# Mirroring the first score group of each sequence into groups 3 to 5 of a fused attention and expert kernel

## The chip, the cores and the metric

One core of one Trainium2 chip runs the whole program. The metric is device time in microseconds of one execution; the time shown for a kernel is the median of several runs.

## What is computed

There are 8 sequences of 2816 tokens with 256 features. Attention has no softmax: squared, rectified scores of `z` with itself weight `v`, and `u` gates the result. The gated rows go to a mixture of experts: a dense two-layer block for every token, and one of eight experts, chosen by the largest logit and weighted by its probability.

```
scores = (1/S) * z @ z.T                  # per sequence, S = 2816, z has 64 features
x      = u * (relu(scores)**2 @ v)        # 22528 x 256 in all
y      = relu(x @ w1_dense) @ w2_dense
e, g   = argmax and its softmax weight of x @ w_gate
out    = y + g * (relu(x @ w1[e]) @ w2[e])
```

The scores of a sequence are a symmetric matrix. A block of it that was computed for keys i and queries j is, turned, the block for keys j and queries i.

## The kernel before

Tokens of a sequence lie in 22 blocks of 128. The query blocks of a sequence form six groups of widths 2, 4, 4, 4, 4, 4, here called 0 to 5; `groups` lists them for all sequences, and `n` counts them through, so that `n % 6` is the place in the sequence. For each group a tile `A[n]` holds the squared scores of all 22 key blocks against the group's queries, in bf16. There are three such tiles in turn (`bufs=3`), so group 3 of a sequence takes the buffer that group 0 had.

- `scores` (matmuls on line 390) makes score steps: for a group of width 4 a step is two key blocks, two matmuls with 64 rows each on the two halves of TensorE. `relu` gives each step two operations after it: an evacuation with scale and relu into `r` (line 405 on ScalarE, 407 on VectorE) and a squaring into `A[n]` (lines 418 and 420). A small list planner (`offer`, `best`, `give`, `run`) puts each on the engine that it expects to be free first; the order on TensorE, ScalarE, VectorE and SyncE is the order in which Python issues the instructions.
- `far[n]` names the groups whose scores group n takes over in place of computing them: before, only group n - 2 of the same sequence. `far_steps` makes the transposing DMA for it (line 468 on SyncE's queue, 16 blocks, or 8 from group 0), `turned_to` says where in `A[n]` it goes, and `block` finds a block again for the multiplication. The steps wait in the list `turning`; `av` takes one from it at fixed points of its loop, once the planner expects the source to be there. `open_group(n)` first carries out all steps of group n - 3, whose buffer it takes.
- `av` multiplies two query blocks of a group with `v` (line 579): 22 key blocks, twice, in pairs of 64-row matmuls. Between them `fill` puts score steps of the group itself or of the next two groups, when a pair of PSUM banks is free (four pairs rotate, `pairs`). `gate_x` (line 606) then multiplies with `u` into `pays` and turns the result by DMA (line 608) for the routing logits (line 634), which come every 11 blocks, five blocks late.
- `load_u` (line 146) loads `u` four blocks ahead on SyncE's queue. `load_z` (line 106) and `load_v` (line 129) are issued from GpSimd's queue, as are the scatters of gated rows (line 724) and the expert weights (`weights`, lines 255 and 259). The weights of all experts stay in one tile `wall`, 2048 columns (`WD`) for each expert. A small VectorE memset ahead of a load decides when it is issued.
- `turn_z` copies half of the next sequence's `z` on VectorE (line 113) and turns it by DMA on SyncE's queue (line 116).
- The table near the end gives ticks to these loads: tick `b * nK + x` is block x of sequence b. Before, the next `z` is loaded at block 0 and turned at blocks 5 and 6, `v` comes at blocks 13 to 18, and the dense and expert weights at blocks 15, 18 and 21, from sequence 1 to 7.

After attention (about 560 us) the experts run tile by tile on rows that were sorted by scatter. That part is not touched.

Of the kernel before, what the change touches and what calls it, by code (L numbers as in the profile page):

```python
# [15 lines left out]
P = 128  # L16
# [3 lines left out]
def kernel(  # L20
# [13 lines left out]
    B, S, D = u.shape  # L34
    dq = z.shape[2]
    E = moe_w_gate.shape[1]
    F = moe_w1_dense.shape[1]
    N = B * S
    assert D == 256 and dq == 64 and F == 512 and E == 8 and S % (2 * P) == 0
    nK = S // P  # L40
# [19 lines left out]
    WD = 2 * F + 4 * D  # L60
# [28 lines left out]
    wall = const.tile([P, E, WD], BF, name="wall")  # L89
# [13 lines left out]
    def load_z(b):  # L103
        z_of[b] = zpool.tile([P, nK, dq], BF, name="zr", bufs=1)
        nc.vector.memset(z_of[b][:, 0, 0:1], 0.0)
        nc.gpsimd.dma_start(out=z_of[b][:], in_=z[b].rearrange("(p k) d -> p k d", p=P))

    def turn_z(b, k0, k1):

        if k0 == 0:  # L110
            zn_of[b] = zpool.tile([P, nK, 2, dq], BF, name="zn", bufs=1)
            zT_of[b] = zpool.tile([P, nK, P], BF, name="zT")
        nc.vector.tensor_copy(
            zn_of[b][:, k0:k1, :, :],
            z_of[b][:, k0:k1, :].unsqueeze(2).to_broadcast([P, k1 - k0, 2, dq]))
        nc.sync.dma_start_transpose(
            out=zT_of[b][:, k0:k1, :],
            in_=zn_of[b][:, k0:k1].rearrange("p k h d -> p (k h d)"))
        if k1 == nK:
            z_there.add(b)  # L120

    def load_v(b, h, parts, gate=True):
        if h == 0:
            v_of[b] = zpool.tile([P, nK, D], BF, name="vb")
        src = v[b].rearrange("(p k) d -> p k d", p=P)
        k0, k1 = h * nK // parts, (h + 1) * nK // parts
        if gate:
            nc.vector.memset(v_of[b][:, k0, 0:1], 0.0)
        nc.gpsimd.dma_start(out=v_of[b][:, k0:k1, :], in_=src[:, k0:k1, :])
        free["pool"] = max(free["pool"], now[0]) + 0.8  # L130
# [133 lines left out]
    A = {}  # L264
    groups = []
# [16 lines left out]
    def offer(ready, rank, ways, then=None):  # L282
        count[0] += 1
        todo.append((rank, count[0], ready, ways, then))
# [56 lines left out]
        run(now[0])  # L341


    left, far, key_at = {}, {}, {}
    for n, (b, i0, w) in enumerate(groups):
        far[n] = [m for m in (n - 2,) if m >= 0
                  if groups[m][0] == b]
        turned = {k for m in far[n] for k in range(groups[m][1], groups[m][1] + groups[m][2])}
        ks = [k for k in range(0, nK, 2) if k not in turned]

        left[n] = [tuple(ks[x:x + 4 // w]) for x in range(0, len(ks), 4 // w)]

    def open_group(n):
        if n not in A:
            while turning and turning[0][0] <= n - 3:
                turning.pop(0)[1]()
            A[n] = aA.tile([P, nK, 4 * P], BF, name="A", tag="A")[:]
            w = groups[n][2]
            if w < 4:
                A[n] = A[n].rearrange("p k c -> p (k c)")[:, :nK * w * P]  # L360
                A[n] = A[n].rearrange("p (k c) -> p k c", k=nK)
# [81 lines left out]
    def turned_to(a, n):  # L443

        _, j0, wj = groups[a]
        w = groups[n][2]
        flat = A[n].rearrange("p k c -> p (k c)")
        return flat[:, j0 * w * P:(j0 + wj) * w * P]

    def block(n, k, c):  # L450

        _, i0, w = groups[n]
        for a in far[n]:
            _, j0, wj = groups[a]
            if j0 <= k < j0 + wj:
                x = c * wj + k - j0
                return turned_to(a, n)[:, x * P:(x + 1) * P]
        return A[n][:, k, c * P:(c + 1) * P]

    def far_steps(a):  # L460

        _, j0, wj = groups[a]

        def step(n):
            _, i0, w = groups[n]
            assert a + 1 in A
            open_group(n)
            nc.sync.dma_start_transpose(
                out=turned_to(a, n).rearrange("p (x c) -> p x c", c=P),
                in_=A[a][:, i0:i0 + w, :].rearrange("p k c -> p (k c)"))  # L470
            turn_at[0] = now[0] + 0.17 * w * wj
            read_at[a] = now[0] + 1.5 + 0.19 * w * wj
            for j in range(wj):
                key_at[n, j0 + j] = now[0] + 7.0

        return [(a, lambda n=n: step(n), n) for n in (a + 2,) if a in far.get(n, [])]

    turning = []
    turn_at = [0.0]
# [73 lines left out]
    def av(n, i, between):  # L553
        b, i0, w = groups[n]
        if i == i0:
            turning.extend(far_steps(n))
# [452 lines left out]
    def at(tick, fn):  # L1009
        later.setdefault(tick, []).append(fn)  # L1010

    def soon(t, fn, dur=0.07):
        at(t, lambda: offer(now[0], 3, {"dve": (dur, lambda eng: fn())}))

    def dense(w, src, c):
        nc.vector.memset(w[:, 0, 0:1], 0.0)
        nc.gpsimd.dma_start(out=w[:], in_=src.rearrange("(c p) f -> p c f", p=P))
# [3 lines left out]
    for b in range(B):  # L1021
        t = b * nK
        if b + 1 < B:
            soon(t, lambda b=b: load_z(b + 1))
            soon(t + 5, lambda b=b: turn_z(b + 1, 0, nK // 2), 0.4)
            soon(t + 6, lambda b=b: turn_z(b + 1, nK // 2, nK), 0.4)
            for h in range(8):
                soon(t + 13 + 5 * h // 7, lambda b=b, h=h: load_v(b + 1, h, 8))

    ts = [b * nK + x for b in range(1, B) for x in (15, 18, 21)][2:]  # L1030
    soon(ts.pop(0), lambda: dense(w1d, moe_w1_dense, 2))
    soon(ts.pop(0), lambda: dense(w2d, moe_w2_dense, 4))
    for e in range(E):
# [62 lines left out]
    for q in range(nQ - 2):  # L1096
        t = starts[q + 1] - 1 + LAG
# [40 lines left out]
    for s in range(NT - MAYBE + 2):  # L1138
# [4 lines left out]
        if s % 3 == 1 and waiting:  # L1143
# [5 lines left out]
    n = nc.values_load(used[0:1, 0:1], min_val=0, max_val=NH,  # L1149
                       skip_runtime_bounds_check_because="made by the table")  # L1150
# [34 lines left out]
```

## Time and profile before

| | before |
|---|---|
| runs | 885.04, 883.94, 883.76 us; median 883.94 us |
| profiled execution | 883.35 us, of it a span of 881.2 us from first to last instruction |
| granted TensorE clock | 0.997 of full speed |
| TensorE / VectorE / ScalarE / GpSimd busy | 861.5 / 700.9 / 737.2 / 491.6 us |
| DMA moved | 127.62 MB, 145 GB/s over the span |
| a sequence in the steady part | 67.43 us |

Busy times are sums over one profiled execution. The queues named SPq and POOLq only issue DMAs; the data moves later on 16 DMA engines that all queues share. A DMA share above 1 means that packets of several queues were under way on one engine at once, their times added.

### The profile page before, as it was taken

To read this page: it belongs to the slowest core of one execution; us is meant where nothing else is said; L and a number is where in the kernel's file an instruction comes from. 1 tells how busy PE (TensorE), PEld (TensorE's weight loads), DVE (VectorE), ACT (ScalarE), POOL (GpSimd) and SP (SyncE) were. 2 spreads that over 40 slices of the span, in tenths; PEclk is the share of its full clock that TensorE was granted. 3 is DMA by queue.
4 is the path that set the end of the run, shared out by engine and by line. 5 is a ranking of instruction groups with operands and counts; after the bars stand their busy time and mean duration, and the time that the engine had idled before them with its cause. 6 is when DMAs were issued, how large, how long until landed. Compare 5 with 4: busy or idle time off the path is not lost.

```text
span 881.2 us, 30493 instructions
## 1 busy us (share of the span) xinstructions
PE 861.5 (98%) x12257; PEld 757.7 (86%) x12257; DVE 700.9 (80%) x1348; ACT 737.2 (84%) x913; POOL 491.6 (56%) x560
## 2 busy tenths in 40 slices
PE   7999999999999999999999999999999999999995
PEld 5788898898888888888888888888888888889994
DVE  7999999998999999999999996756665445446663
ACT  7999998998998998998998994577777777777773
POOL 8203355445426436436336334588888888877664
PEclk9999999999999999999999999999999999999998
DMA  8897988979979979989999976465646565533442
GB/s 155 148 151 139 161 162 149 185 165 173 181 161 185 167 165 185 162 181 143 198 182 165 165 135 115 104 136 131 136 122 120 121 123 122 124 103 103 95 98 76
DMA packets 258830, 127.62 MB, mean 145 GB/s; under 512 B 222846, under 2 KB 237438, under 8 KB 258688
## 3 DMA queue, kind: packets, MB, share of 16 engines
q1 hardware_dynamic: 227040, 70.23, 46.2%
q0 software_dynamic: 31648, 55.45, 29.6%
q8 instruction: 96, 1.57, 0.8%
q14 instruction: 46, 0.38, 0.1%
HBM read 61.54 MB, written 37.16 MB: 112 GB/s over the span
## 4 chain that ended last, share of the span: by engine, by line
PE 81%; POOL 6%; issue 4%; DVE 4%; DMA 2%; ACT 1%; SPq 0%; POOLq 0%; DVEq 0%; ACTq 0%
PE o L579 44%; PE h_ps L936 13%; PE yy L944 12%; PE s L390 10%; POOL out_dram L962 5%; DMA out_dram<-ring,ix 1%; DVE r L407 1%; PE lg L634 1%; POOL A L420 1%; DVE A L420 1%; ACT r L405 1%; DMA ring<-xs 1%; DVE pays L606 0%; ACT A L418 0%; DMA z<-in_z_dram 0%
## 5 line engine op out<-in xcount | busy, mean ns | idle before, releaser
L579 PE MATMUL o<-vb,A 64*128 64x256 bf16 x7744 | 491.1, 269 | 3.3 <-POOL A L420 1.7
L579 PEld LDWEIGHTS <-A 64*128 64x128 bf16 x7744 | 406.5, 94 | 53.7 <-POOL A L420 3.0
L724 POOL DMA_INDIRECT xs<-pays,pi x176 | 190.2, 1081 | 249.3 <-DVE pi L722 204.5
L405 ACT ACTIVATE r<-s 128x1024 f32<-128x1024 f32 (+1 forms) x268 | 263.8, 1012 | 21.6 <-PE s L390 19.2
L418 ACT ACTIVATE A<-r 128x1024 bf16<-128x1024 f32 (+1 forms) x263 | 266.6, 1046 | 7.1 <-DVE r L407 4.2
L939 ACT ACTIVATE ring<-h_ps 128x1024 bf16<-128x1024 f32 x180 | 184.1, 1024 | 89.6 <-PE h_ps L936 88.1
L407 DVE TENSOR_SCALAR r<-s 128x1024 f32<-128x1024 f32 (+1 forms) x164 | 197.6, 1215 | 6.5 <-PE s L390 1.9
L420 DVE TENSOR_TENSOR A<-r 128x1024 bf16<-128x1024 f32 x161 | 196.4, 1231 | 2.1 <-ACT r L405 1.7
L960 DVE SCALAR_TENSOR_TENSOR ring<-yy,me,ring 128x256 f32<-128x256 f32 x180 | 86.9, 483 | 124.6 <-ACT ring L959 84.7
L962 POOL DMA_INDIRECT out_dram<-ring,me x140 | 147.5, 1054 | 42.0 <-issue 24.4
L390 PE MATMUL s<-zT 64*128 64x512 bf16 (+1 forms) x944 | 156.8, 357 | 1.8 <-ACT zT L192 0.6
L944 PEld LDWEIGHTS <-ring 128*128 128x128 bf16 x1440 | 140.1, 98 | 16.1 <-issue 0.3
L944 PE MATMUL yy<-w2d,ring 128*128 128x256 bf16 x720 | 108.0, 273 | 0.1
L944 PE MATMUL yy<-ring 128*128 128x256 bf16 x720 | 108.0, 273 | 0.0
L936 PE MATMUL h_ps<-ring,w1d 128*128 128x256 bf16 x720 | 93.3, 272 | 1.0 <-DVE pays L606 0.8
L936 PE MATMUL h_ps<-ring 128*128 128x256 bf16 (+1 forms) x880 | 93.7, 253 | 0.0
L924 DVE COPY ring<-wall 128x2048 bf16 x110 | 79.7, 740 | 8.0 <-DVE ring L960 4.0
L936 PEld LDWEIGHTS <-ring 128*128 128x128 bf16 x880 | 74.3, 98 | 6.8
L936 PEld LDWEIGHTS <-w1d 128*128 128x128 bf16 x720 | 70.1, 98 | 9.3 <-issue 1.0
L390 PEld LDWEIGHTS <-zT 64*128 64x128 bf16 x944 | 57.6, 94 | 16.5 <-issue 2.6
L606 DVE TENSOR_TENSOR pays<-o,ut 128x512 bf16<-128x512 f32 x88 | 60.4, 687 | 14.0 <-PE o L579 13.7
L959 ACT COPY ring<-yy 128x256 f32<-128x256 f32 x180 | 65.9, 366 | 1.8 <-PE yy L944 1.8
(120 smaller groups left out, 370.0 us busy)
## 6 DMA issues: line engine op xcount, KB each, us to landing
ut<-in_u_dram SPq DMA_DIRECT2D x88, 256.0 KB
vb<-in_v_dram POOLq DMA_DIRECT2D x42, 192.0 KB
wall<-in_moe_w_dram POOLq DMA_DIRECT2D x16, 256.0 KB
xs<-pays,pi POOLq DMA_INDIRECT x176
zr<-in_z_dram POOLq DMA_DIRECT2D x7, 352.0 KB
out_dram<-ring,me POOLq DMA_INDIRECT x140
ring<-xs SPq DMA_TRANSPOSE x114
vb<-in_v_dram POOLq DMA_DIRECT2D x14, 128.0 KB
```

The costliest lines, as they stand in the source:

```text
L390: nc.tensor.matmul(out=s[:, h, y * c:(y + 1) * c], lhsT=zT[r, k + h, :], rhs=zT[r, i0:i0 + w, :], start=True, stop=True)
L405: nc.scalar.activation(r[:, :, :c], s[:, :, :c], AF.Relu, scale=1.0 / S)
L407: nc.vector.tensor_scalar(out=r[:, :, :c], in0=s[:, :, :c], scalar1=1.0 / S, scalar2=0.0, op0=ALU.mult, op1=ALU.max)
L418: nc.scalar.activation(a, r, AF.Square)
L420: (nc.gpsimd if eng == "pool" else nc.vector).tensor_mul(a, r, r)
L579: nc.tensor.matmul(out=o[:, j, 0:D], lhsT=block(n, k, i + j - i0)[r], rhs=v_of[b][r, k, :], start=(p == 0 and x == 0), stop=(p == 1 and x ...
L724: ins = nc.gpsimd.indirect_dma_start(out=xs, out_offset=bass.IndirectOffsetOnAxis(ap=pi[:], axis=0), in_=pays[:, g % (2 * G), 0:ROW].bitca ...
L936: nc.tensor.matmul(out=h_ps[:, f, hs, :], lhsT=w1(c, f), rhs=xT[:, hs, c, :], start=(c == 0), stop=(c == 1))
L939: nc.scalar.activation(h, h_ps[:].rearrange("p f h t -> p f (h t)"), AF.Relu)
L944: nc.tensor.matmul(out=y[:, k, :], lhsT=h[:, f, j * P:(j + 1) * P], rhs=w2(f), start=(f == 0), stop=(f == 3))
L960: nc.vector.scalar_tensor_tensor(out=ys, in0=y[:, 1, :], scalar=me[:, j, 0:1], in1=yd, op0=ALU.mult, op1=ALU.add)
L962: ins = nc.gpsimd.indirect_dma_start(out=out, out_offset=bass.IndirectOffsetOnAxis(ap=ids[j], axis=0), in_=ys, in_offset=None, bounds_chec ...
```

## The change

For every sequence but the last, the scores that group 0 computed (its two query blocks) are now turned into groups 3, 4 and 5 too, besides group 2, which had them before. Groups 3 to 5 then have one score step fewer each. `A` keeps its size: the three turned pieces, 128 x 1024 each, go into the columns of `wall` that belong to the last expert and to the second half of the one before. Those weights are loaded in the last sequence, at blocks 4, 9 and 14, when no mirror is made any more; the earlier weights keep their order. `z` of the next sequence is loaded three blocks sooner, at block 19 of the sequence before (at block 0 for the first), and turned at blocks 0 and 1 (5 and 6 in the first sequence).

```diff
+    spare = wall[:].rearrange("p e w -> p (e w)")
+    mirror = {(0, 4): (E - 1) * WD, (0, 5): (E - 1) * WD + 8 * P, (0, 3): (E - 2) * WD + 2 * F}
+
+    def slots(b):
+
+        return list(mirror) if b < B - 1 else []
...
-        far[n] = [m for m in (n - 2,) if m >= 0
-                  if groups[m][0] == b]
+        far[n] = [m for m in range(max(n - 5, 0), n - 1)
+                  if groups[m][0] == b and (m == n - 2 or (m % 6, n % 6) in slots(b))]
...
-        flat = A[n].rearrange("p k c -> p (k c)")
-        return flat[:, j0 * w * P:(j0 + wj) * w * P]
+        if a == n - 2:
+            flat = A[n].rearrange("p k c -> p (k c)")
+            return flat[:, j0 * w * P:(j0 + wj) * w * P]
+        x = mirror[a % 6, n % 6]
+        return spare[:, x:x + w * wj * P]
...
-            assert a + 1 in A
-            open_group(n)
+            if n == a + 2:
+                assert a + 1 in A
+                open_group(n)
...
-        return [(a, lambda n=n: step(n), n) for n in (a + 2,) if a in far.get(n, [])]
+        return [(a, lambda n=n: step(n), n) for n in range(a + 2, min(a + 6, len(groups)))
+                if a in far[n]]
...
-            soon(t, lambda b=b: load_z(b + 1))
-            soon(t + 5, lambda b=b: turn_z(b + 1, 0, nK // 2), 0.4)
-            soon(t + 6, lambda b=b: turn_z(b + 1, nK // 2, nK), 0.4)
+            soon(max(t - 3, 0), lambda b=b: load_z(b + 1))
+            tz = t if b else 5
+            soon(tz, lambda b=b: turn_z(b + 1, 0, nK // 2), 0.4)
+            soon(tz + 1, lambda b=b: turn_z(b + 1, nK // 2, nK), 0.4)
...
-    ts = [b * nK + x for b in range(1, B) for x in (15, 18, 21)][2:]
+    ts = [b * nK + x for b in range(1, B - 1) for x in (15, 18, 21)][2:-1]
+    ts += [(B - 1) * nK + x for x in (4, 9, 14)]
```

More of the change, by code (lines that the diff above doesn't have):

```diff
@@ L1023 @@
         if b + 1 < B:
-            soon(t, lambda b=b: load_z(b + 1))
-            soon(t + 5, lambda b=b: turn_z(b + 1, 0, nK // 2), 0.4)
-            soon(t + 6, lambda b=b: turn_z(b + 1, nK // 2, nK), 0.4)
+            soon(max(t - 3, 0), lambda b=b: load_z(b + 1))
+            tz = t if b else 5
+            soon(tz, lambda b=b: turn_z(b + 1, 0, nK // 2), 0.4)
+            soon(tz + 1, lambda b=b: turn_z(b + 1, nK // 2, nK), 0.4)
             for h in range(8):
                 soon(t + 13 + 5 * h // 7, lambda b=b, h=h: load_v(b + 1, h, 8))
-    ts = [b * nK + x for b in range(1, B) for x in (15, 18, 21)][2:]
+    ts = [b * nK + x for b in range(1, B - 1) for x in (15, 18, 21)][2:-1]
+    ts += [(B - 1) * nK + x for x in (4, 9, 14)]
+    assert len(ts) == 2 + 2 * E
     soon(ts.pop(0), lambda: dense(w1d, moe_w1_dense, 2))
```

## The prediction

> **What bounds the kernel now.** I read the page first (busy shares, the chain that ended last, the groups), then the waits of TensorE, then the busy time per stretch of one sequence, and last the single queues around the place where a sequence begins. The page:
>
> ```profile
> PE 861.5 (98%) x12257; PEld 757.7 (86%) x12257; DVE 700.9 (80%) x1348; ACT 737.2 (84%) x913; POOL 491.6 (56%) x560
> DMA  8897988979979979989999976465646565533442
> PE 81%; POOL 6%; issue 4%; DVE 4%; DMA 2%; ACT 1%; SPq 0%; POOLq 0%; DVEq 0%; ACTq 0%
> ...
> L579 PE MATMUL o<-vb,A 64*128 64x256 bf16 x7744 | 491.1, 269 | 3.3 <-POOL A L420 1.7
> ...
> L405 ACT ACTIVATE r<-s 128x1024 f32<-128x1024 f32 (+1 forms) x268 | 263.8, 1012 | 21.6 <-PE s L390 19.2
> L418 ACT ACTIVATE A<-r 128x1024 bf16<-128x1024 f32 (+1 forms) x263 | 266.6, 1046 | 7.1 <-DVE r L407 4.2
> ...
> L407 DVE TENSOR_SCALAR r<-s 128x1024 f32<-128x1024 f32 (+1 forms) x164 | 197.6, 1215 | 6.5 <-PE s L390 1.9
> L420 DVE TENSOR_TENSOR A<-r 128x1024 bf16<-128x1024 f32 x161 | 196.4, 1231 | 2.1 <-ACT r L405 1.7
> ...
> L390 PE MATMUL s<-zT 64*128 64x512 bf16 (+1 forms) x944 | 156.8, 357 | 1.8 <-ACT zT L192 0.6
> ```
>
> TensorE is busy 98% and holds 81% of the chain. The reader should see that its two attention groups have almost no idle time ahead of them (3.3 and 1.8 us in all), while ScalarE and VectorE, which turn scores into A, wait for it: 19.2 us of ACT's idle ends with a score. One sequence, in the steady stretches, beside the expert half (first column the stretch, then its length):
>
> ```profile
> core 0: us, PE busy (x) PEld busy (x) DVE busy (x) ACT busy (x) POOL busy (x), PEclk, DMA share, GB/s
> 253.79:321.22 67.43, 67.34 (x1150) 58.83 (x1148) 64.07 (x119) 63.30 (x70) 30.16 (x34) 1.00 0.93 173
> 388.65:456.08 67.43, 67.34 (x1150) 58.84 (x1148) 64.06 (x119) 63.30 (x70) 30.05 (x34) 1.00 1.04 172
> 560.00:881.00 321.00, 310.90 (x3009) 280.06 (x3007) 179.62 (x387) 228.57 (x357) 247.94 (x288) 0.99 0.51 115
> ```
>
> A sequence takes 67.43 us, 67.34 of them TensorE at full clock. So attention is bound by TensorE, with VectorE (64.07) and ScalarE (63.30) 5 to 6% behind. A stall of either for more than a moment stops TensorE, and the DMA share is near or over 1. The change touches attention alone; the expert stretch after 560 us keeps its 321 us.
>
> **What is removed.** In each of the first seven sequences, groups 3, 4 and 5 no longer compute the score step of key blocks 0 and 1: 3 x 7 = 21 steps, each two 64x512 matmuls that run beside each other, one evacuation with relu and one squaring. The order of the built program bears this out: 42 matmuls `s<-zT` fewer, 14 evacuations and one squaring fewer on DVE, 7 and 20 fewer on ACT. The matmul's mean of 357 ns is no price, since pairs overlap. The chain, piece by piece, has it:
>
> ```profile
> 258.68 0.22 PE s L390 x2
> 258.90 1.75 PE o L579 x32
> 260.64 0.22 PE s L390 x2
> ```
>
> A pair holds the chain for 0.22 us (a pair of A-times-v matmuls 1.75/16 = 0.109). So TensorE loses 21 x 0.22 = 4.6 us of work, or 0.66 us per sequence. On ACT and DVE 21 steps of about 2.14 us go (263.8+266.6+197.6+196.4 over 432 steps), 45 us in all. That is worth nothing by itself: those engines already wait for TensorE, which has only 0.09 us of idle left per sequence. Multiplying costs what it did: the same 7744 matmuls are issued, and 336 of them read the mirror instead of A.
>
> **What is added.** 21 transposing DMAs of 128x1024 on SP's queue (8 blocks, 262 kB each). In before's trace group 0's one transpose and what stands around it on SP, with the long transposes of group 1:
>
> ```profile
> 287.12 0.34 SPq L146 DMA_DIRECT2D ut<-in_u_dram  x1
> 287.56 1.23 SPq L608 DMA_TRANSPOSE xT<-pays  x1
> 288.89 1.29 SPq L468 DMA_TRANSPOSE A<-A  x1
> ...
> 296.00 4.26 SPq L468 DMA_TRANSPOSE A<-A  x1
> 300.35 0.54 SPq L146 DMA_DIRECT2D ut<-in_u_dram  x1
> ```
>
> Now four transposes come out of A of group 0 instead of one. Two DMAs that turn z, until now at blocks 5 and 6, move between them, and in the program's order group 1's transpose follows at once. What waits for that: (a) SP: group 1's transpose writes the buffer of group 0 and so waits until all four have read it, with the next u and xT behind it; u is asked for four blocks early and xT is used five blocks late, some 12 us each (67.43/22 a block), so this costs nothing below that. (b) ACT and DVE: group 3 uses group 0's buffer, so their first squaring into it waits for the last mirror. Behind it on ACT is the evacuation of the next score, and TensorE's routing logits take the PSUM pair which that frees. This is the one place where the change can cost TensorE time. (The mirrored keys are not needed before group 3 multiplies, over 10 us later.)
>
> I lay (b) out from the u load that opens this burst (time 0), placing each issue by the TensorE work ahead of it in the built program (0.109 and 0.22 as above). SP: u 0.3, xT 1.2, two mirrors of 1.29, to 4.2; half of z's turn waits for its copy on DVE and ends at about 5.8; mirror three to 7.1; u and xT of the next pair to 8.7; the last mirror is issued from 8.8 to 10.1. The data cannot come much faster than DMA moves it. The price of that, from half-microseconds around a 16-block transpose that has SP and DMA nearly to itself:
>
> ```profile
> 307.02 2.16 SPq L468 DMA_TRANSPOSE A<-A  x1
> ...
> 307.50:308.00 0.50, 0.50 (x9) 0.18 (x6) 0.43 (x3) 0.50 (x1) 0.08 (x1) 1.00 1.26 245
> 308.00:308.50 0.50, 0.50 (x10) 0.41 (x10) 0.50 (x1) 0.50 (x2) 0.50 (x1) 1.00 1.20 223
> ...
> 310.00:310.50 0.50, 0.50 (x14) 0.44 (x12) 0.46 (x4) 0.41 (x2) 0.00 (x0) 1.00 1.19 214
> 311.00:311.50 0.50, 0.50 (x14) 0.44 (x12) 0.50 (x2) 0.50 (x2) 0.50 (x1) 1.00 0.25 42
> ```
>
> That is about 230 GB/s, starting about 1 us after the issue. Ahead of the last mirror's end lie two u (524 kB), two xT (328), four mirrors (1049), half of z (360), one weight half (262) and two or three scatters (some 200), by their shapes: 2.7 MB, or 11.7 us. From 0.9 on that ends at 12.6. In ACT's own order the first squaring into group 3 starts at 13.3, and the logits follow its end by one evacuation, with another 0.2 us free. So the margin is about 0.9 us. It is thin, and the row at 296.00 (4.26 us for an issue that elsewhere takes 2.16) shows that SP is held back in this very stretch when other loads are under way. Bounds for (b) per sequence: nothing (all four gone at SP's pace, at 11.1), and about 1.7 us (SP held by 2.1 more, as at 296.00, on top of the 12.6, is 1.2 us over the edge at 13.5; half a microsecond more for a scatter in between). No end below nothing, as TensorE has nothing else to win there. I take 0.1 us per sequence, 0.7 in all, since the sum by bytes ends ahead of the edge.
>
> [...]
>
> **What is moved.** z's load goes from block 0 of a sequence to block 19 of the one before, behind the v loads and two weight halves on POOL's queue; its copy on DVE waits for it, now about 6 us after the issue instead of 22:
>
> ```profile
> 1.28 2.64 DMA z<-in_z_dram
> ...
> 291.29 0.58 POOL L106 DMA_DIRECT2D zr<-in_z_dram  x1 [0.18 <-issue]
> ...
> 313.32 0.88 DVE L113 COPY zn<-zr 128x1408 bf16<-128x1408 bf16 x1
> ```
>
> The nearest rows bound its landing by 2.6 us (a first, smaller z load with DMA empty) and 22 us (before's slack). I take 2.6 plus 360 kB at 230 GB/s, 4.2 us: nothing, as it fits in 6. The copies of 0.88 us move within DVE's row and are the same number. Three weight halves come in the last sequence, where no mirror is made, against two before; they land long before their experts. Nothing.
>
> **Sum.** The profiled execution took 883.35 us (span 881.2), 0.6 under the median of 883.94. 883.35 - 4.6 + 0.7 = 879.4; from the median the same sum gives 880.0, which is my forecast.
>
> **Rivals.** *The last mirror lands late.* ACT's first squaring into group 3 waits, the logits wait behind it, and TensorE stops in each of seven sequences. Against it: the 0.9 us margin. For it: the DMA shares of 0.93 to 1.04, the 4.26 us issue, and 24 more blocks to turn in each sequence (before it is 133: 56 of A, 55 of x, 22 of z). At 1.5 us per sequence: 883.94 - 4.6 + 10.5 = 889.8, slower. It eats the gain at 0.66 us per sequence and counts as slower from (4.6 + 1.8)/7 = 0.9. [...]
>
> *The gain is eaten, no more.* The same wait at 0.4 to 0.9 us per sequence, 882.2 to 885.7: no difference that can be told.
>
> *z comes late.* With v and weights ahead of it on the same queue, z lands 2 us after DVE asks; DVE, with evacuations and the gate behind it, has 3.4 us spare per sequence but TensorE has only the free PSUM pairs of about 1 us. About 1 us in six sequences: 883.94 - 4.6 + 6 + 0.7 = 886.0, slower. Against it: before's v loads and z together had 22 us and no wait is seen; the load now follows the last v load by some 3 us.
>
> **How the numbers follow.** A measurement of this kernel tells about 0.2%, 1.8 us, from no change. My forecast (under 0.36 us lost per sequence, 878.5 to 882.1) has 0.60. The gain eaten has 0.14. The late mirror over 0.9 us has 0.20, late z 0.06: slower 0.26. The low end is the sum from the profiled execution with nothing lost (878.7), rounded down. The high end reaches into the slow cases to 886.5, 1 us lost in each sequence, which leaves out somewhat over one in ten above. The forecast's own range is 878.5 to 882.1.
>
> **What would show it.** Steady sequences of 66.8 us, TensorE still within 0.2 us of all of it, and the score group at x902. Where I am wrong, TensorE's waits gain a row of logits or scores behind ACT, ACT's squaring shows idle time that ends with the DMA `A<-A` or `wall<-A` (late mirror), or DVE's copy of z shows idle time that ends with z's DMA (late z). If sequences are shorter by more than 0.66 us, or not at all with no such wait, the price of a score pair is wrong.

## The result and the profile after

| | before | after |
|---|---|---|
| median of the runs | 883.85 us (883.26 to 885.04, 4 runs) | 924.75 us (923.68 to 929.31, 4 runs) |
| ratio | | 1.0471, 95% interval 1.0433 to 1.0509 |
| profiled execution, span | 883.35, 881.2 us | 929.31, 927.5 us |
| granted TensorE clock | 0.997 | 0.974 |
| last multiplication of attention starts | 554.1 us | 600.7 us |

The change costs 41 us where 4 us of gain were forecast. Ratios here and below leave out runs more than 1.5% above the fastest of the same kernel, which were two, both of e9. The profiled execution after is the slowest of its four, 46.0 us above the profiled one before. From its page the busy sums, the clock by fortieths of the span, the chain's shares and two groups:

```profile
PE 875.4 (94%) x12216; PEld 763.5 (82%) x12216; DVE 684.1 (74%) x1333; ACT 713.6 (77%) x886; POOL 493.5 (53%) x560
...
PEclk9999899899999989989989999999999999999998
...
PE 55%; DMA 7%; POOL 6%; issue 6%; DVE 5%; ACT 2%; SPq 0%; POOLq 0%; DVEq 0%; ACTq 0%
...
L425 ACT ACTIVATE A<-r 128x1024 bf16<-128x1024 f32 x243 | 249.2, 1046 | 41.0 <-DMA wall<-A 18.6
...
L397 PE MATMUL s<-zT 64*128 64x512 bf16 (+1 forms) x902 | 153.7, 365 | 6.8 <-DVE r L414 2.0
```

The work went as planned (x902 score matmuls; ScalarE and VectorE are busy for less), but TensorE fell from 81% of the chain to 55% and DMA rose from 2% to 7%; ScalarE's squaring (now line 425) has 18.6 us of idle time that ends with a DMA into `wall`. The stretches of attention and of the experts:

```profile
36.00:600.70 564.70, 529.07 (x8735) 456.00 (x8733) 472.19 (x892) 450.90 (x492) 225.07 (x245) 0.96 0.94 159
606.00:927.00 321.00, 311.38 (x3017) 280.58 (x3014) 179.39 (x389) 228.88 (x358) 247.10 (x288) 0.99 0.48 115
```

The part after the last multiplication of attention is as long as before (927.5 - 600.7 = 326.8 us, and 881.2 - 554.1 = 327.1), so the loss is all in attention. There TensorE is idle for 564.70 - 529.07 = 35.6 us. The same stretch of the kernel before, to the end of its attention:

```profile
36.00:554.00 518.00, 515.12 (x8776) 450.27 (x8774) 487.90 (x907) 474.56 (x519) 222.31 (x245) 1.00 0.93 164
```

There it was 2.9 us. TensorE's clock is also lower now: (1 - clock) times busy time, added up over stretches of 1 us, is 18.5 us, against none before. 32.7 us more idle and 18.5 of clock, less the 4.6 us of dropped work, is 46.6 us, which is by how much attention ends later. The waits, with total, times and longest:

```profile
PE lg L646 <- ACT r L412: 24.5, 6, 4.7
ACT A L425 <- DMA wall<-A: 18.6, 4, 5.0
...
DVE zn L113 <- DMA zr<-in_z_dram: 8.9, 4, 3.4
...
ACT A L425 <- issue: 7.9, 2, 4.5
```

Six times TensorE's logits (line 646) wait 4 us on average for an evacuation that is queued on ScalarE behind a squaring, and that squaring waits for a mirror. One burst shows the order, SyncE's queue first, then ScalarE and the chain:

```profile
158.96 0.33 SPq L146 DMA_DIRECT2D ut<-in_u_dram  x1
...
160.69 2.84 SPq L479 DMA_TRANSPOSE A<-A  x1
163.58 3.76 SPq L479 DMA_TRANSPOSE wall<-A  x1
167.43 2.66 SPq L116 DMA_TRANSPOSE zT<-zn  x1
170.18 1.27 SPq L479 DMA_TRANSPOSE wall<-A  x1
171.54 1.29 SPq L146 DMA_DIRECT2D ut<-in_u_dram  x1
...
174.19 1.26 SPq L479 DMA_TRANSPOSE wall<-A  x1
...
177.64 3.52 SPq L479 DMA_TRANSPOSE A<-A  x1
```
```profile
177.60 1.06 ACT L425 ACTIVATE A<-r 128x1024 bf16<-128x1024 f32 x1 [3.44 <-issue]
178.56 1.92 ACT L412 ACTIVATE r<-s 128x1024 f32<-128x1024 f32 x2
```
```profile
179.62 0.73 PE lg L646 x22
180.35 0.97 PE o L591 x8
181.32 0.43 PE s L397 x2
```

The last mirror is issued at 174.19, 15.2 us after the u load. ScalarE's first squaring into group 3 (177.60) and group 1's transpose (177.64) start together: both wait for that mirror to have read group 0's buffer, 18.6 us after the u load. The profile calls ScalarE's 3.44 us "issue" here and "DMA wall<-A" in four other sequences. In the six bursts after the first sequence the last mirror is issued 12.3 to 18.0 us after the u load, and group 1's transpose, which waits for its reading, starts at 17.6 to 22.0. And the score pair that follows holds the chain for 0.43 us, not 0.22. The clock column of this stretch (third from the right) says why:

```profile
174.00:176.00 2.00, 2.00 (x38) 1.75 (x33) 2.00 (x4) 0.16 (x1) 1.59 (x1) 1.00 1.06 259
176.00:178.00 2.00, 0.29 (x6) 0.10 (x2) 0.47 (x2) 0.40 (x1) 1.08 (x2) 1.00 0.98 179
178.00:180.00 2.00, 0.38 (x15) 0.38 (x15) 0.40 (x1) 2.00 (x3) 0.00 (x0) 0.78 1.23 192
180.00:182.00 2.00, 2.00 (x30) 1.35 (x28) 1.86 (x6) 1.75 (x4) 0.00 (x0) 0.50 1.10 204
```

TensorE stands still for 3.3 us, and then works at half clock until 186 us.

### The profile page after: what moved, and what is told of

It reads as the page before. It is cut to its first block, busy times and chain, and to the rows that moved or that the text cites. A ratio compares the mean times of both kernels' runs of the same rounds, so it can differ in the third digit from the quotient of the medians.

```text
span 927.5 us, 30392 instructions
## 1 busy us (share of the span) xinstructions
PE 875.4 (94%) x12216; PEld 763.5 (82%) x12216; DVE 684.1 (74%) x1333; ACT 713.6 (77%) x886; POOL 493.5 (53%) x560
## 4 chain that ended last, share of the span: by engine, by line
PE 55%; DMA 7%; POOL 6%; issue 6%; DVE 5%; ACT 2%; SPq 0%; POOLq 0%; DVEq 0%; ACTq 0%
PE o L591 25%; PE h_ps L948 12%; PE yy L956 12%; POOL out_dram L974 5%; PE s L397 5%; DMA xs<-pays,pi 2%; DMA wall<-A 2%; DVE r L414 2%; DMA out_dram<-ring,ix 1%; DVE A L427 1%; DMA wall<-in_moe_w_dram 1%; ACT r L412 1%; ACT A L425 1%; PE lg L646 1%; DVE pays L618 1%
## 5 line engine op out<-in xcount | busy, mean ns | idle before, releaser
L591 PE MATMUL o<-vb,A 64*128 64x256 bf16 x7408 | 482.7, 274 | 3.3 <-ACT A L425 1.4
L591 PEld LDWEIGHTS <-A 64*128 64x128 bf16 x7408 | 395.2, 96 | 56.8 <-issue 6.1
L736 POOL DMA_INDIRECT xs<-pays,pi x176 | 192.7, 1095 | 300.8 <-DVE pi L734 262.9
L412 ACT ACTIVATE r<-s 128x1024 f32<-128x1024 f32 (+1 forms) x261 | 255.9, 1010 | 57.2 <-PE s L397 54.5
L425 ACT ACTIVATE A<-r 128x1024 bf16<-128x1024 f32 x243 | 249.2, 1046 | 41.0 <-DMA wall<-A 18.6
L427 DVE TENSOR_TENSOR A<-r 128x1024 bf16<-128x1024 f32 (+1 forms) x160 | 193.0, 1219 | 26.8 <-ACT r L412 26.3
L414 DVE TENSOR_SCALAR r<-s 128x1024 f32<-128x1024 f32 (+1 forms) x150 | 181.1, 1214 | 10.9 <-PE s L397 8.3
L974 POOL DMA_INDIRECT out_dram<-ring,me x140 | 148.4, 1060 | 42.0 <-issue 24.4
L397 PE MATMUL s<-zT 64*128 64x512 bf16 (+1 forms) x902 | 153.7, 365 | 6.8 <-DVE r L414 2.0
L618 DVE TENSOR_TENSOR pays<-o,ut 128x512 bf16<-128x512 f32 x88 | 60.4, 687 | 39.5 <-PE o L591 38.0
L397 PEld LDWEIGHTS <-zT 64*128 64x128 bf16 x902 | 55.5, 95 | 26.1 <-issue 12.9
```

The lines of the kernel that those rows point to most:

```text
L397: nc.tensor.matmul(out=s[:, h, y * c:(y + 1) * c], lhsT=zT[r, k + h, :], rhs=zT[r, i0:i0 + w, :], start=True, stop=True)
L412: nc.scalar.activation(r[:, :, :c], s[:, :, :c], AF.Relu, scale=1.0 / S)
L414: nc.vector.tensor_scalar(out=r[:, :, :c], in0=s[:, :, :c], scalar1=1.0 / S, scalar2=0.0, op0=ALU.mult, op1=ALU.max)
L425: nc.scalar.activation(a, r, AF.Square)
L427: (nc.gpsimd if eng == "pool" else nc.vector).tensor_mul(a, r, r)
L591: nc.tensor.matmul(out=o[:, j, 0:D], lhsT=block(n, k, i + j - i0)[r], rhs=v_of[b][r, k, :], start=(p == 0 and x == 0), stop=(p == 1 and x ...
```

## The experiments

The runs fell on chips on which the kernel before takes 884 us and on others with 930 us, so each ratio is against the kernel before on the same chip, over the runs and not from the two medians. e1 and e16 are one kernel on the two kinds of chip: of the 47.8 us between their spans 39.0 lie behind attention and 8.8 in it. No execution of the kernel before was profiled on a 930 us chip. "Idle" and "clock" are TensorE's from 36 us to the end of attention in the profiled execution, worked out as above (before: 2.9 and none; after: 35.6 and 18.5 us). By e1 and e16 some 5 us of idle belong to the 930 us chips.

| experiment | us (before) | ratio, 95% interval | idle, clock |
|---|---|---|---|
| e1: steps dropped, no mirror DMAs | 924.48 (930.07) | 0.9928, 0.9901 to 0.9954 | 7.5, 0 |
| e2: mirrors, z as before | 951.73 (930.07) | 1.0194, 1.0135 to 1.0254 | 25.4, 5.2 |
| e3: only z moved | 933.19 (930.07) | 1.0039, 1.0007 to 1.0071 | 9.9, 0 |
| e4: mirror DMAs, nothing dropped | 971.58 (930.07) | 1.0442, 1.0395 to 1.0490 | 33.6, 13.6 |
| c5: the whole change again | 928.48 (883.44) | 1.0481, 1.0438 to 1.0525 | 40.6, 14.1 |
| e6: same DMAs, another source | 889.77 (883.44) | 1.0078, 1.0056 to 1.0099 | 7.5, 3.4 |
| e7: e2, group 3 held 12 us | 885.96 (883.44) | 1.0025, 0.9998 to 1.0053 | 8.0, 1.6 |
| e8: z loaded still sooner | 896.53 (883.44) | 1.0138, 1.0121 to 1.0155 | 16.6, 5.0 |
| e9: e2, group 3 held 18 us | 883.78 (883.67) | 0.9988, 0.9961 to 1.0014 | 7.6, 0 |
| e10: no z or weights in the burst | 907.93 (883.67) | 1.0273, 1.0246 to 1.0300 | 21.0, 8.1 |
| e11: e10, held 12 us | 882.46 (883.67) | 0.9989, 0.9976 to 1.0002 | 6.4, 0 |
| e12: before, with short pauses | 899.40 (883.67) | 1.0180, 1.0163 to 1.0196 | 15.7, 0 |
| e13: e10, z turned earlier | 924.64 (931.00) | 0.9933, 0.9902 to 0.9964 | 6.6, 0 |
| e14: e13, held 12 us | 924.21 (931.00) | 0.9902, 0.9864 to 0.9939 | 7.1, 1.7 |
| e15: before, with longer pauses | 975.21 (931.00) | 1.0456, 1.0414 to 1.0499 | 39.5, 13.4 |
| e16: e1 on the 884 us chip | 878.03 (883.82) | 0.9933, 0.9908 to 0.9958 | 2.5, 0 |
| e17: e14 on the 884 us chip | 880.13 (883.82) | 0.9956, 0.9940 to 0.9973 | 2.0, 0 |

### Which part costs it: e1 to e4

e1 drops the steps and issues no mirror from the second sequence on:

```diff
+                if n > a + 2 and a >= 6:
+                    for j in range(wj):
+                        key_at[n, j0 + j] = now[0] + 7.0
+                else:
+                    steps.append((a, lambda n=n: step(n), n))
```

> The 21 score steps are gone as in the change, but from the second sequence on the mirror DMAs are left out (groups 3 to 5 multiply the mirror of the first sequence, so this part of the scores is replaced), and z is loaded and turned at its old blocks. All theories: if a score pair is worth 0.22 us of TensorE, 883.9 - 4.6 = 879 to 880 us and steady sequences of 66.8 us. If the shorter work itself upsets the order (rival), 884 or more.

e2 is the change with z's three lines put back (load at block 0, turned at 5 and 6).

> The whole change but z: loaded at block 0, turned at blocks 5 and 6 as before. Theory A (the last mirror lands late because z's copy and turn stand in SP's row between the mirrors; the stall then halves TensorE's clock for some 6 us): most of the loss goes, 880 to 890 us, TensorE clock back to 0.99. Theory B (the four transposes by themselves are too much for the DMA engines at that place): 905 to 925 us, the wait of ACT for wall<-A stays at 3 us or more per sequence.

e3 is the kernel before with z's new lines alone.

> The kernel before with z alone moved (loaded at block 19 of the sequence before, turned at blocks 0 and 1), no mirror. Theory A: z's copy on VectorE waits 1 to 3 us for its load in most sequences, 886 to 900 us. Theory B: no loss, 883 to 885 us. Theory C (late z is the whole loss): 915 us or more.

e4 computes all scores as before, z as before, and issues the mirrors into the spare columns, where nobody reads them:

```diff
+        def extra(n):
+            ...
+            nc.sync.dma_start_transpose(
+                out=spare[:, x:x + w * wj * P].rearrange("p (x c) -> p x c", c=P),
+                in_=A[a][:, i0:i0 + w, :].rearrange("p k c -> p (k c)"))
+        if a % 6 == 0 and groups[a][0] < B - 1:
+            steps += [(a, lambda n=n: extra(n), n) for n in range(a + 3, a + 6)]
```

> The kernel before with the 21 mirror DMAs added (and the weights loaded as in the change), but nobody reads them: all score steps are computed, z at its old blocks. Theory A: 884 to 895 us. Theory B: 910 to 930 us, with ACT or VectorE waiting for wall<-A as in the change.

Dropping the steps gains 0.7% (the forecast's 4.6 us are 0.5%, inside the interval). The mirrors alone, saving nothing, cost 4.4%; with their saving they cost 1.9%; z alone costs 0.4%. So the transfers are the loss, and z adds to it: 1.9% and 0.4% apart, 4.7% together, though these two stood on a 930 us chip and the change on an 884 us one. e2 fits neither of its theories: 1.9% is some 901 us where before takes 884, between the 890 of the one and the 905 of the other. The waits of e2 between 36 and 555 us:

```profile
DVE A L427 <- DMA wall<-A: 17.4, 5, 4.3
ACT A L425 <- DMA wall<-A: 13.2, 6, 5.8
```

The squaring waits for a mirror with z at its old place too. In one burst of e2, on SyncE's queue:

```profile
232.18 0.33 SPq L146 DMA_DIRECT2D ut<-in_u_dram  x1
...
235.20 6.21 SPq L479 DMA_TRANSPOSE wall<-A  x2
...
243.52 3.07 SPq L479 DMA_TRANSPOSE wall<-A  x1
249.81 2.11 SPq L479 DMA_TRANSPOSE A<-A  x1
```

Two mirrors hold SyncE for 6.21 us, the last is issued 11.3 us after the u load, and group 1's transpose comes free after 17.6 us. So without z's turn in between SyncE is only some 2 us late, but the data is later: in e2's six bursts the last mirror goes out at 9.6 to 11.3 us and the buffer comes free 5.8 to 11.5 us after that, against 3.3 to 5.3 in the change. A weight half (233.60) and z's load (237.68) were issued in this stretch from GpSimd's queue.

### The wait or the traffic: c5, e6

c5 is the change once more, to stand on the same chip as e6 to e8.

> The change itself once more, beside the three kernels below on one chip. It should be slower than before by 3 to 6%. It is there so that each of the others has its reference on the same chip.

e6 issues the same DMAs at the same places, but they read a zeroed part of `wall`, so that group 0's buffer is free after its one old transpose; groups 3 to 5 multiply zeros there:

```diff
+    nc.vector.memset(wall[:, E - 2, 0:2 * F], 0.0)
...
-                in_=A[a][:, i0:i0 + w, :].rearrange("p k c -> p (k c)"))
+                in_=A[a][:, i0:i0 + w, :].rearrange("p k c -> p (k c)") if n == a + 2
+                else wall[:, E - 2, 0:2 * F])
```

> The change with the same 21 transposes at the same places and of the same size, but they read a zeroed piece of the weights' space instead of group 0's scores (so those scores are replaced by zeros). Group 3's first squaring then waits only for the one transpose into group 2. Theory A (the wait for group 0's buffer stops TensorE): nearly all of the loss goes, 0.99 to 1.005 of before, with only the waits for z left. Theory B (the transposes load the DMA engines so that everything is late): still over 1.02.

The ratio falls from 1.048 to 1.008 with every byte still moved. No wait for `wall<-A` is left in its trace. So about five sixths of the loss is the wait for group 0's buffer; against e16, which drops the same steps, it is 4.0 of 5.5%. The 1.5% that is left by that count is traffic and late z together, and e6 stays a little above the 1.005 that the first theory allowed. Late z is still there:

```profile
DVE zn L113 <- DMA zr<-in_z_dram: 6.9, 2, 3.5
```

### Holding group 3 back, or z sooner: e7, e8, e9

e7 is e2 with one number changed: the planner takes group 0's buffer to be read 12 us after a mirror's issue, and so fills other groups' steps in the meantime. e9 says 18 us.

```diff
-            read_at[a] = now[0] + 1.5 + 0.19 * w * wj
+            read_at[a] = now[0] + (12.0 if n > a + 2 else 1.5 + 0.19 * w * wj)
```

> The mirrors with z at its old blocks, and the planner told that group 0's buffer is read until 12 us after the last mirror (3 us in the change), so that group 3's first scores stand later in every engine's row and multiplications stand there instead. Theory A: no engine waits for the mirror any more, 0.990 to 1.000 of before. Theory B: still over 1.015, since the transfers are late for other uses too.

> As the kernel that holds group 3 back until 12 us after the last mirror, but 18 us. In the 12 us one a few squarings still waited 2 to 3 us for the mirror. Theory A: those go too, 0.990 to 0.998 of before. If instead the scores of group 3 now come too late for its multiplications (rival), TensorE waits for ACT or VectorE in that group and it is no better, 1.000 to 1.010.

e8 is the change with z loaded ten blocks ahead instead of three.

```diff
-            soon(max(t - 3, 0), lambda b=b: load_z(b + 1))
+            soon(max(t - 10, 0), lambda b=b: load_z(b + 1))
```

> The change with z loaded ten blocks sooner instead of three (still turned at blocks 0 and 1). If the late copy of z is what makes the change so much worse than the mirrors with z at its old place (it stands ahead of two mirrors on SP), VectorE's wait for z goes and the time comes down to that of the mirrors with old z, 1.01 to 1.025 of before. If it is the turn of z itself, its two transposes between the mirrors, that adds to the burst, it stays at 1.035 to 1.05.

Holding group 3 brings e2's 1.9% (on another chip) down to 0.25% and to nothing that can be told (the runs of both spread over 12 to 15 us); both had been expected a little better. It moves the squaring behind the mirror, but some waits stay (in e9 still 7.1 us on VectorE), and the gain of the dropped steps is spent; on what, no run shows. e8 has no wait for z left and is at 1.4% instead of 4.8%; its last mirrors go out at 11.6 to 13.4 us. So over two thirds of the loss in the change hangs on when z is loaded. That z in time lets SyncE go on to the mirrors behind it is one reason; that the load's own traffic has left the burst may be another, and e8 does not part them. Neither edit is faster than the kernel before.

### A burst without loads: e10, e11, e13, e14

e10 keeps the mirrors and takes z and the weights out of the burst: z is loaded 6 blocks into the sequence and turned at 11 and 12, weights come at blocks 9, 14, 17. e11 holds group 3 back 12 us besides.

```diff
+            soon(t + (6 if b else 0), lambda b=b: load_z(b + 1))
+            soon(t + (11 if b else 5), lambda b=b: turn_z(b + 1, 0, nK // 2), 0.4)
+            soon(t + (12 if b else 6), lambda b=b: turn_z(b + 1, nK // 2, nK), 0.4)
...
+    ts = [b * nK + x for b in range(1, B - 1) for x in (9, 14, 17)][2:-1]
```

> The mirrors as in the change with no hold, but nothing from POOL's queue except scatters comes into the burst at a sequence's start: z is loaded at block 6 and turned at 11 and 12, the weights come at blocks 9, 14 and 17. If the casting loads are what slows the transposes there (193 GB/s over the burst instead of the 230 of a quiet stretch, with pauses of 1.5 us), the mirror lands some 4 us sooner and it comes to 0.993 to 1.003 of before. If SP's u, x and mirrors alone are too much, it stays at 1.015 to 1.02 as with z at its old place.

> Both: no POOL loads in the burst, and group 3 held back until 12 us after the last mirror. Theory A: the whole gain of the dropped score steps, 0.992 to 0.996 of before (876 to 880 us where before is 883.5).

e10 was slower than before by 2.7%, but not for the mirrors. Its waits between 36 and 555 us:

```profile
PE s L397 <- DMA zT<-zn: 18.2, 6, 3.6
...
DVE A L427 <- DMA wall<-A: 0.2, 1, 0.2
```

The mirror's wait is gone (0.2 us in all, against 30.6 in e2). The new one comes with e10's own edit: z turned at blocks 11 and 12 is late for the next sequence's first scores. e11 turns z at the same blocks, but has only 4.5 us of this wait; why holding group 3 back shortens it no run shows, and its 0.9989 misses the 0.992 to 0.996 that was expected. One burst of e10 on SyncE's queue:

```profile
225.39 0.33 SPq L146 DMA_DIRECT2D ut<-in_u_dram  x1
...
228.42 3.61 SPq L479 DMA_TRANSPOSE wall<-A  x2
...
234.00 1.43 SPq L479 DMA_TRANSPOSE wall<-A  x1
```

The last mirror is issued 8.6 us after the u load (8.1 to 9.5 in the six bursts). That is in time, but not the predicted pace: the 8.8 of the prediction had 1.6 us of z's turn in it, which this burst hasn't, so its prices would give 7.2 here. e13 mends z: loaded at block 3, turned at 6 and 7, with the weights at 12, 15 and 18. e14 is that with group 3 held back 12 us.

> As the kernel without POOL loads in the burst (no hold), but z is loaded at block 3, right behind the burst, and turned at blocks 6 and 7, so that the next sequence's first scores don't wait for it; weights at blocks 12, 15 and 18. Theory A (the casting loads in the burst made the last mirror late): no wait for wall<-A and none for zT, 0.993 to 1.000 of before. If the burst of transposes alone were enough, 1.015 or more.

> The same with group 3 held back until 12 us after the last mirror. Theory A: 0.990 to 0.996 of before, the whole worth of the dropped steps. If holding back costs by itself, a little above the kernel without hold.

Both are faster than before, as expected; the two are not told apart. e2 and e13 differ in where z and the weights are loaded and z turned, and nothing else: 1.9% slower becomes 0.7% faster.

### The clock: e12, e15

e12 is the kernel before; in each of the six middle sequences a matmul waits for a GpSimd copy of 900 or 2040 columns. e15 has two copies in a row, of 1300 or 2040 columns.

```diff
...
+        nc.gpsimd.tensor_copy(wall[:, E - 2, 0:size], wall[:, E - 1, 0:1].to_broadcast([P, size]))
+        nc.tensor.matmul(out=d[:], lhsT=wall[0:dq, E - 2, 0:P], rhs=ones[0:dq, 0:8], start=True, stop=True)
...
+        if i == 9 and 0 < b < B - 1:
+            rest_pe((900, 2040)[b % 2])
```

> The kernel before with a pause of TensorE at block 9 of sequences 1 to 6: a tiny matmul waits for a GpSimd copy that was released just before, some 2 us in sequences 2, 4 and 6, some 4 us in sequences 1, 3 and 5 (a few columns of weights' space, loaded later, are written). It prices the clock: if only the longer pauses bring the granted clock to 0.5 for about 6 us, each costs some 3 us beyond itself, and the time is 18 us of pauses plus 9 of clock, 908 to 915 us. If pauses cost their own length alone, 898 to 905 us.

> The kernel before with longer pauses of TensorE at block 9 of sequences 1 to 6: two GpSimd copies in a row, some 3.3 us in sequences 2, 4 and 6, some 4.7 us in 1, 3 and 5. The pauses of 1.2 and 2.6 us left the clock at 1.00 and cost their own length. If the clock falls only after a longer pause, the granted clock goes to 0.5 for 3 to 7 us after the 4.7 us pauses at least, and the time is some 24 us of pauses plus 9 to 18 of clock, 915 to 927 us. If the clock has nothing to do with the pause, 908.

One pause of e12 and one of e15, in stretches of 2 us:

```profile
114.00:116.00 2.00, 1.00 (x19) 0.71 (x13) 2.00 (x4) 1.80 (x3) 0.84 (x2) 1.00 1.11 215
116.00:118.00 2.00, 0.37 (x7) 0.35 (x9) 2.00 (x3) 0.85 (x1) 1.84 (x2) 1.00 0.46 106
118.00:120.00 2.00, 2.00 (x36) 1.71 (x32) 1.91 (x3) 1.63 (x2) 1.51 (x1) 1.00 0.67 148
```
```profile
118.00:120.00 2.00, 0.00 (x0) 0.00 (x0) 2.00 (x1) 0.40 (x1) 1.84 (x2) 1.00 0.41 82
120.00:122.00 2.00, 0.00 (x0) 0.00 (x0) 0.05 (x1) 0.00 (x0) 2.00 (x2) 0.88 0.96 209
122.00:124.00 2.00, 1.15 (x11) 0.76 (x13) 0.00 (x0) 0.00 (x0) 0.80 (x1) 0.50 1.07 221
...
126.00:128.00 2.00, 2.00 (x24) 1.57 (x20) 1.17 (x2) 2.00 (x3) 0.00 (x0) 0.50 0.00 0
128.00:130.00 2.00, 2.00 (x31) 1.55 (x29) 1.19 (x2) 1.31 (x2) 0.00 (x0) 0.91 0.00 0
```

All six pauses of e12 (1.4 to 2.7 us, 12.5 in all) left the clock at 1.00, and the kernel grew by 15.7 us. All six of e15 (5.0 to 6.6 us, 34.7 in all) were followed by 0.50, worth 1.5 to 2.8 us each, 13.4 in all, and the kernel grew by 44.2. The pauses came out shorter in e12 and longer in e15 than planned (18 and 24 us), so the expected times say little; the price of the clock lies in its expected 9 to 18. No mirror or late z is in either. So the stall itself brought the half clock on where it was 5.0 us or longer. It added 0.4 of the stalls' length in e15; in the change the six long stalls (24.5 us) drew 15.3 us of it, 0.6 of their length.

### On a chip where the kernel before takes 884 us: e16, e17

> The 21 score steps gone, the mirroring DMAs left out from the second sequence on, z at its old place, as in the first run; groups 3 to 5 there multiply what lies in the spare columns. The other run of it was on a chip where the kernel before takes 930 us, 46 us of it in the expert part. Prediction's step (a score pair is worth 0.22 us of TensorE, 21 of them): 4.6 us less, ratio 0.9948, on any chip. Rival (the gain there came from that chip alone, where attention before has more idle time than the 2.9 us seen here): under 2 us, 0.998 or more, where before takes 884 us.

> All four mirrors, group 3 held back 12 us, z loaded at block 3 and turned at 6 and 7, weights at 12, 15, 18. Theory (late mirrors and their stalls are the whole loss): the gain of the dropped steps is kept within 2 us of the run without mirrors, so a ratio within 0.003 of that one. Rival (the mirrors' traffic costs besides the stalls): 0.4% or more above it.

e16 gains 5.8 us: the price of a score pair holds there too, a little over the 4.6 (its expectation puts 46 us of the other chip's time into the expert part; it is 39). e17 keeps 3.7 of that with all four mirrors made and read, 0.23% above e16, and is the version that beats both kernels. Its burst, and its attention to 545 us:

```profile
151.34 0.33 SPq L146 DMA_DIRECT2D ut<-in_u_dram  x1
...
155.32 2.86 SPq L479 DMA_TRANSPOSE wall<-A  x2
...
160.16 1.27 SPq L479 DMA_TRANSPOSE wall<-A  x1
164.69 1.32 SPq L479 DMA_TRANSPOSE A<-A  x1
```
```profile
36.00:545.00 509.00, 507.13 (x8672) 447.08 (x8669) 466.60 (x880) 451.96 (x491) 238.97 (x243) 1.00 1.06 176
```

In this burst the last mirror goes out 8.8 us after the u load and the buffer is free at 13.35 or sooner; over the six bursts it goes out at 8.8 to 12.9, later than in e13 (8.4 to 9.4), and the hold covers that. TensorE lacks 1.9 us in 509, at full clock. Its last multiplication of attention starts at 549.7 us, 4.4 before that of the kernel before.

## Why the prediction was wrong

**What held.** TensorE bounds attention (in the kernel before it is busy for 515.1 of the 518.0 us shown above); a dropped pair is worth about 0.22 us (e16: 5.8 us less, 4.6 forecast; both e1 and e16 have 4.6 inside their interval); x902; the order on SyncE's queue; that losing ScalarE and VectorE work gains nothing by itself (in e16's attention they are busy for 24.4 and 17.5 us less, for the 5.8 gained); that (b) is the one place where the mirrors can stop TensorE, by the path named: squaring, evacuation, logits. The rival of the late mirror is what came true, with its named marks in the waits.

**The step that failed: the landing of the last mirror.** The prediction had it issued 8.8 us after the u load and read by 12.6, against an edge at 13.5. In the burst shown it was issued at 15.2 and read by 18.6; ScalarE was itself ready only at 15.2, so it waited 3.4 us and not 5.1. After the issue it took 3.4 us, as reckoned (3.8; 3.3 to 5.3 in the six bursts); the miss lies ahead of it, on SyncE. The first two transposes took 2.84 and 3.76 us where twice 1.29 was charged (4.0 us), z's turn 2.75 from the mirror before it to its end where 1.6 was (1.2), and the u load 1.29 where 0.33 was (1.0). These prices were taken from rows where SyncE had room, the mirrors at the 1.29 of one transpose alone, and the data at 230 GB/s from quiet half-microsecond rows. The burst itself moved 183 GB/s:

```profile
159.00:177.60 18.60, 15.83 (x259) 13.77 (x255) 15.59 (x21) 12.50 (x13) 6.51 (x7) 1.00 1.18 183
```

The prediction quoted the row that told this, 4.26 us at 296.00 for a transpose that elsewhere takes 2.16, and charged it once, in a bound, as 2.1 us on top. Of a margin of 0.9 us that left the bound at 1.7 us per sequence; the waits of the logits were 24.5 us in six, 4.1 each. In e10 and e17, without z and weights in the burst, the last mirror went out at 8.6 and 8.8 in the bursts shown, before the edge; with z's turn taken out the prediction's prices give 7.2, so they are some 1.5 us short even there.

**z.** The load was reckoned to land 4.2 us after its issue, with its copy due after some 6, and priced at nothing. VectorE waited for it four times, up to 3.4 us. The larger cost need not be on VectorE: half of z's turn stands on SyncE ahead of mirrors three and four, so late z can make the mirror late; the last one goes out at 12.3 to 18.0 us in the change, 11.6 to 13.4 in e8 with z in time, 9.6 to 11.3 in e2 without z's turn there. The prediction listed the two rivals apart and gave each its own price; the runs add up otherwise (1.9% and 0.4% on one chip, 4.7 and 4.8% together on two others). A wait placed between two others that share a queue must be priced with them.

**The clock.** No step had a price for TensorE running slower after a stall; 18.5 us of the loss in the profiled execution is that. e15 shows it without the change. The granted clock falls to 0.50: every stall of 3.3 us or more in the change, e4 and e15 brought that, none of e12's up to 2.7 us. Between 1.4 and 3.1 us both occur: the change at 241 us did, e2 at 463 us did not. The traces tell these apart. In each of the ten runs with half clock in attention, the clock changes there only on a grid of 3.41 us (in the change it falls at 104.02, 179.12 and 243.96 us, 22 and 19 steps apart), and half clock lasts one or two steps, 3.41 or 6.83 us (once four, 13.7 us in e4). The two places, cut along that grid, the change first:

```profile
240.55:243.96 3.41, 1.19 (x19) 0.82 (x14) 3.41 (x4) 0.49 (x2) 0.00 (x0) 1.00 1.62 71
243.96:247.37 3.41, 3.13 (x26) 2.16 (x27) 3.41 (x7) 2.55 (x3) 1.82 (x2) 0.50 1.35 209
```
```profile
461.03:464.45 3.42, 2.00 (x36) 1.54 (x31) 1.87 (x3) 1.06 (x1) 0.30 (x1) 1.00 0.26 52
464.45:467.86 3.41, 1.98 (x30) 1.47 (x31) 3.27 (x8) 2.38 (x4) 0.66 (x1) 1.00 0.97 199
```

One step with 2.2 us of standstill was followed by the half; two with 1.4 us each were not. In the attention of all runs 41 steps at full clock were followed by the half. In 40 of them TensorE stood still for 1.87 us or more, in one for 1.43; no step with more than 1.90 stayed without it. So here a step need not be idle throughout: 1.87 us of its 3.41 were enough (in the change, the step from 390.75 us). A second step of half clock followed wherever TensorE stood still for 1.0 us or more of the first, as in e15 from 121.5 to 128.4 us (1.3 us), and nowhere at under 0.39 us.

**What stays open.** What holds SyncE in the crowded burst. In one burst of e2, after a half-microsecond with a DMA share of 4.75, the rows show 0, 7 and 58 GB/s around 240 us. But these columns count a packet wholly where it begins; 4.75 over half a microsecond is 2.4 us of packets for each of the 16 engines, so in the rows behind it they were still busy with packets begun before (an estimate, from that sum). Nor does a share above 1 need several queues, other than what stands ahead of the prediction: in the kernel before, the packets of the hardware queue q1 alone come to a share of 1.38 from 500 to 502 us. That the z and weight loads and the transposes share the engines (in the change, from 158 to 178 us, the packets of q0, the queue of the loads, took 33% of the 16 engines' time and those of q1, the queue of the transposes, 80%) goes with it, and taking them out cured it in e13, but loads and weights were not taken out one by one. e4 cost more than e2 (4.4% and 1.9%), more than its undropped steps of 0.7% explain; no run settles why.

## What to carry to other kernels

Where a new reader is added to a buffer that rotates, the cost is the time of its last read, on the fullest stretch of the queue: take each transfer's price from a row of that stretch, not from a quiet one, and treat a margin of less than one held-back issue as no margin. In these runs a stall of TensorE cost about its length (12.5 us of pauses made e12 15.7 us longer), and the half clock, where it followed, 1.5 to 3.2 us more: it came behind none of e12's up to 2.7 us, behind some of 1.4 to 3.1 us elsewhere, behind every one of 3.3 us and more. By the 1.9 us and the 3.41 us grid above, one of 3.8 us draws it wherever it falls (an estimate). A transfer that must end early wants the other loads moved out of its burst, and the planner told when it really ends: that turned +4.7% into -0.4%.

## What the runs showed of the hardware

In attention the clock granted to TensorE changed only on a grid of 3.41 us (41 falls in ten runs). It fell to 0.50 behind a step in which TensorE stood still for some 1.9 us or more (once 1.43), so after every stall of 3.3 us and more and after some of 1.4 to 3.1 us, and mostly stayed there for 3.4 or 6.8 us; the price, 1.5 to 3.2 us a time in the change, comes on top of the stall. A transposing DMA of 8 blocks took 1.29 us of SyncE's queue in the kernel before (at 288.89 us). In the burst of the change shown, with weights loaded in it, it took 1.26 to 3.76 us, and two took 6.21 in that of e2 (in e17's, with z and weight loads out of it, 2.17 for one and 2.86 for two); one such issue of the change, at 238.58 us, took 6.95:

```profile
238.58 6.95 SPq L479 DMA_TRANSPOSE wall<-A  x1
```

The same kernel took 884 us on some chips and 930 on others; by e1 and e16, some four fifths of the difference lie behind attention.
